# Stationary operands read with a step of two words, in a kernel of pooled attention and two feed-forward layers

## The chip, the cores and the metric

The kernel runs on one core of one Trainium2 chip. The metric is device time in microseconds (us) of one execution; the kernel before took 976.43 us, the median of three runs (975.0 to 977.66). The engines are PE (TensorE: PE for products, PEld for the loads of their stationary operands), DVE (VectorE), ACT (ScalarE), POOL (GpSimd) and SP (which issues DMAs here). L741 means line 741 of the kernel before.

## The reference

`x` has 12480 tokens of 128 channels; 32 inducing rows attend to all tokens, the tokens attend to the 32 pooled rows, and two feed-forward layers of 2048 hidden units follow. The weights are float64, all else is float32.

```python
def mab(q, kv):
    s = scale * (q @ kv.transpose(0, 2, 1))
    a = np.exp(s - s.max(-1, keepdims=True))
    a /= a.sum(-1, keepdims=True) + 1e-09
    return a @ kv
h = mab(I, x)                       # 32 pooled rows
x = mab(x, h).reshape(12480, 128)   # tokens
h = x @ moe_w_in                    # 128 x 2048
x = np.maximum(0.01 * h, h) @ moe_w_out
h = x @ moe2_w_in
return (h * (1.0 / (1.0 + np.exp(-1.702 * h)))) @ moe2_w_out
```

## The kernel before, in words

**Halves.** A float32 product is made of passes over halves in float32r, a four-byte type: `hi` holds a value's upper 12 significant bits, `lo` the rest. A product of two such values takes three passes (hi hi, lo hi, hi lo). In each pass one operand is stationary (128 x 128, loaded into PE ahead of the product) and one is moving (up to 512 columns that stream through).

**Tiles.** The tokens are cut into 25 tiles, 23 of 512 columns and the first and last of 352. The 2048 hidden units are cut into NF = 16 blocks of 128. A step is one block of one tile. The list `steps` holds first all 400 steps of the first layer (the first two tiles interleaved, four blocks at a time), then the 400 of the second. Step n issues `ffn_in` and `ffn_act` of its block, `ffn_out` of the block three steps before (LOOK = 3), and then the work that `extra` has put at this step.

**First layer.** The tokens' attention is folded into the first weights: `hw` is the product of the pooled rows and `moe_w_in`, stacked as (hi, hi, lo, lo) on the partitions' four quadrants, against the attention weights `at` as (hi, lo, hi, lo). So `ffn_in` is one product (L709, stationary `hw`). `ffn_act` makes `ghi` on ACT (L723) and `glo` on DVE (L724). `ffn_out` is three products (L741, L742, L743) with stationary blocks of `v1`, hi, lo and hi. At the end of a tile comes one product with `lin` (L745), the linear part of the leaky unit.

**Second layer.** `ffn_in` is three products (L713, L714, L715) with stationary column blocks of `w2`, hi, lo and hi; `ffn_act` is two activations on ACT (L729, L730) and a subtraction on DVE (L731); `ffn_out` is the same three products with blocks of `v2`.

**Weights.** Each weight matrix arrives as float64 bits in four blocks of 128 x 512 values. `convert_stages` makes float32 halves of one block: a load on SP's queue, magnitude on ACT (L134), clamp on POOL (L137), shift, top and bottom on DVE (L140, L145, L150; the last two read every second word of `raw`), and upper: `hi` on ACT (L155) and `lo` on POOL (L156). `matrix_in` has hi and lo in two tiles; `matrix_out` keeps a block's 128 hi words and then its 128 lo words. `w1` is only a moving operand (in `pooled_block`, L638); `v1`, `w2`, `v2` and `hw` are stationary. w1 and v1 are converted before and beside the first two tiles, w2 from step 60 on (in w1's place), v2 from step 160 on.

**hw.** `pooled_block` makes 512 columns of `hw` in PSUM, `pooled_upper` writes the hi rows (L619, ACT), `pooled_lower` the lo rows (L623, DVE), four times (b = 0 to 3). `linear_transposed` transposes hw's blocks on PE (L657), `linear_product` multiplies them with `v1` (L667), `linear_copy` and `linear_end` sum the parts into `lin`.

**Order.** It is written out by hand (`tc.manual_schedule()`): each engine runs its instructions in the order in which the program issues them, and the tables at the file's head (CONV, POOLED, LINEAR, GROUP) say at which step the work beside the layers is put. `keep_busy` issues products of zeros (bf16, 256 columns, L106) where PE would stand.

Of the kernel before, what the change touches and what calls it, by code (L numbers as in the profile page):

```python
# [10 lines left out]
F32 = mybir.dt.float32  # L11
# [7 lines left out]
P = 128  # L19
LOOK = 3  # blocks of hidden units between both products  # L20
TC = 4  # chunks of tokens in a token tile
ENDS = 88  # tokens of a chunk in the first and the last tile, 128 in the others
B = 32  # side of VectorE's transposed blocks
# [5 lines left out]
# pieces of x that blocks of weights are loaded before, the iterations of their conversion  # L29
W_LOADS = [6, 8]  # L30
W_STEPS = [0, 0, 1, 2, 2, 3]
# where the work beside the first two tiles goes, by their steps
# [14 lines left out]
def kernel(  # L47
# [10 lines left out]
    """float32 products run as float32r passes over halves: hi is a value's upper 12  # L58
    significant bits, lo = value - hi the others, both exact in float32r."""
# [23 lines left out]
    # token p * chunks + j of a part of x is row p of chunk j  # L83
# [4 lines left out]
    # token tiles that are loaded together  # L88
# [14 lines left out]
    def keep_busy(count):  # L103
        """TensorE's clock halves when it waits for long: products of zeros meanwhile."""
        for _ in range(count):
            nc.tensor.matmul(  # L106
                idle_ps[:, :256], idle[:, :P], idle[:, :256], start=True, stop=True
            )

# [1 line left out]
    CW = 512  # L111
    LOW = bits_f32(896 << 20)  # the words of 2^-127 and of float32's largest 2^127 * f
    HIGH = bits_f32((1150 << 20) | 0xFFEFF)

    def convert_stages(src, hi, lo):
        """src: [P, CW] of float64 bits. Its magnitude clamped to float32's range, sign,
        exponent and 23 fraction bits make a float32: hi is its rounding, lo the rest."""
# [42 lines left out]
    def matrix_in(src, name, tag):  # L160
        """[model, hidden]: a column block of hidden units is a stationary operand."""
        hi, lo = (wts.tile([P, DFF], F32R, name=f"{name}{h}", tag=f"{tag}{h}") for h in "hl")
# [6 lines left out]
    def matrix_out(src, name):  # L169
        """[hidden, model] by blocks of hidden units, hi and lo of a block side by side."""  # L170
        w = wts.tile([P, NF, 2, C], F32R, name=name)
        parts = []
        for o in range(0, DFF, CW):
            f = slice(o // P, (o + CW) // P)
            s = src[o : o + CW, :].bitcast(U32).rearrange("(f p) d -> p f d", p=P)
            parts.append((s, w[:, f, 0, :], w[:, f, 1, :]))
        return w, parts

    w1, w1_parts = matrix_in(moe_w_in, "w1", "w")
    v1, v1_parts = matrix_out(moe_w_out, "v1")  # L180

# [703 lines left out]
```

## Time and profile before

| | |
|---|---|
| runs | 976.43 us median (975.0, 976.43, 977.66) |
| profiled execution | span 974.8 us; its time beyond the span isn't listed, the runs' median is 1.6 us above it |
| PE busy | 963.9 us (99%), 4630 products |
| PEld busy | 783.3 us (80%), 4630 loads |
| ACT busy | 787.8 us (81%) |
| DVE busy | 644.5 us (66%) |
| POOL busy | 67.2 us (7%) |
| granted PE clock | full (2.4 GHz) in all 40 slices |
| first layer | from 47.9 us (first L709) to 433.7 us (last L745) |
| second layer | from 430.8 us (first L713) to the end |

Busy times of PE come from modelled ends, since products are pipelined: the end of one lies behind the start of the next. The distance from start to start is what a product costs in a sequence. The rows give a start, a duration, the engine, the line, the operation, out<-in by the program's names, the shape, a count, and in brackets the idle time before it with what ended it.

### The profile page before, as it was taken

The numbers are of one execution on the slowest core, as the hardware profiler recorded it, in microseconds if no ns is written. First come the engines' busy times: TensorE is split into PE (matmuls) and PEld (weight loads), VectorE is DVE, ScalarE is ACT, GpSimd is POOL, SyncE is SP. The second block draws the span as 40 slices with busy tenths as digits, with TensorE's granted clock in tenths as the row PEclk, the third lists the DMA queues.
The fourth block names the chain that finished last, engine by engine and source line by source line (L and its number), as shares of the span: only waits on it lengthen the run. The fifth ranks groups of instructions, "written<-read, shape, count | busy, mean of one in ns | idle before, by whom it ended". The sixth has DMA issues, their size and how long they took to land.

```text
span 974.8 us, 13366 instructions
## 1 busy us (share of the span) xinstructions
PE 963.9 (99%) x4630; PEld 783.3 (80%) x4630; DVE 644.5 (66%) x1049; ACT 787.8 (81%) x1378; POOL 67.2 (7%) x53
## 2 busy tenths in 40 slices
PE   9989999999999999999999999999999999999998
PEld 6667787887878878898888888888888888888887
DVE  4898788978878778765555555555555555555554
ACT  6576677767766666679999999999999999999997
POOL 1360021202200000000000000000000000000000
PEclk9999999999999999999999999999999999999999
DMA  9302120031000100000000000000000000000000
GB/s 340 98 1 55 33 65 22 7 93 33 23 23 7 27 12 23 8 1 8 12 11 12 11 12 22 11 11 11 12 12 12 11 11 18 16 12 12 12 11 19
DMA packets 15434, 27.99 MB, mean 29 GB/s; under 512 B 2358, under 2 KB 6870, under 8 KB 15366
## 3 DMA queue, kind: packets, MB, share of 16 engines
q1 hardware_dynamic: 15366, 27.14, 8.8%
q8 instruction: 36, 0.59, 0.2%
q14 instruction: 32, 0.26, 0.1%
HBM read 14.79 MB, written 6.39 MB: 22 GB/s over the span
## 4 chain that ended last, share of the span: by engine, by line
PE 96%; DVE 3%; DMA 0%; ACT 0%; issue 0%; SPq 0%; DVEq 0%; ACTq 0%
PE acc L743 18%; PE acc L742 18%; PE acc L741 18%; PE h_ps L715 9%; PE h_ps L713 9%; PE h_ps L714 9%; PE h_ps L709 9%; PE xT_ps L255 1%; DVE glo L724 1%; PE s_ps L272 1%; PE s_ps L563 1%; PE pv_ps L321 1%; PE acc L745 1%; PE p_ps L302 1%; DMA xn<-in_x_dram 0%; DVE v L145 0%
## 5 line engine op out<-in xcount | busy, mean ns | idle before, releaser
L731 DVE TENSOR_TENSOR glo<-g,ghi 128x512 fp32r<-128x512 f32 (+1 forms) x400 | 271.7, 679 | 238.9 <-ACT ghi L730 226.9
L723 ACT ACTIVATE ghi<-h_ps 128x512 fp32r<-128x512 f32 (+1 forms) x400 | 233.1, 587 | 101.6 <-PE h_ps L709 97.1
L743 PE MATMUL acc<-glo,v 128*128 128x512 f32 (+1 forms) x800 | 310.6, 388 | 0.8 <-DVE glo L724 0.6
L742 PE MATMUL acc<-ghi,v 128*128 128x512 f32 (+1 forms) x800 | 309.1, 386 | 0.5 <-POOL v L156 0.5
L741 PE MATMUL acc<-ghi,v 128*128 128x512 f32 (+1 forms) x800 | 308.2, 385 | 0.0
L724 DVE SCALAR_TENSOR_TENSOR glo<-h_ps,ghi 128x512 fp32r<-128x512 f32 (+1 forms) x400 | 263.4, 674 | 65.1 <-ACT ghi L723 61.7
L729 ACT ACTIVATE g<-h_ps 128x512 f32<-128x512 f32 (+1 forms) x400 | 234.8, 587 | 36.2 <-PE h_ps L715 0.5
L730 ACT ACTIVATE ghi<-g 128x512 fp32r<-128x512 f32 (+1 forms) x400 | 248.2, 620 | 12.6
L742 PEld LDWEIGHTS acc<-ghi,v 128*128 128x128 f32 x800 | 150.3, 188 | 33.5 <-POOL v L156 0.8
L743 PEld LDWEIGHTS acc<-glo,v 128*128 128x128 f32 x800 | 150.3, 188 | 33.2 <-DVE glo L724 3.5
L741 PEld LDWEIGHTS acc<-ghi,v 128*128 128x128 f32 x800 | 150.3, 188 | 28.6
L715 PE MATMUL h_ps<-x2l,w2h 128*128 128x512 f32 (+1 forms) x400 | 156.8, 392 | 0.0
L709 PE MATMUL h_ps<-at,hw 128*128 128x512 f32 (+1 forms) x400 | 155.4, 389 | 0.3 <-ACT at L543 0.3
L713 PE MATMUL h_ps<-x2h,w2h 128*128 128x512 f32 (+1 forms) x400 | 154.7, 387 | 0.0
L714 PE MATMUL h_ps<-x2h,w2l 128*128 128x512 f32 (+1 forms) x400 | 153.1, 383 | 0.0
L709 PEld LDWEIGHTS h_ps<-at,hw 128*128 128x128 f32 x400 | 75.1, 188 | 20.1 <-issue 3.6
L714 PEld LDWEIGHTS h_ps<-x2h,w2l 128*128 128x128 f32 x400 | 75.1, 188 | 16.1
L715 PEld LDWEIGHTS h_ps<-x2l,w2h 128*128 128x128 f32 x400 | 75.1, 188 | 15.6
L713 PEld LDWEIGHTS h_ps<-x2h,w2h 128*128 128x128 f32 x400 | 75.1, 188 | 15.5
L137 POOL TENSOR_SCALAR v<-v 128x512 f32<-128x512 f32 x16 | 31.7, 1983 | 59.3 <-ACT v L134 59.3
L759 ACT ACTIVATE x<-acc 128x512 f32<-128x512 f32 (+1 forms) x25 | 14.7, 587 | 7.7 <-PE acc L745 7.7
L762 DVE TENSOR_SCALAR o_t<-acc 128x512 f32<-128x512 f32 (+1 forms) x25 | 16.8, 671 | 0.5 <-PE acc L743 0.5
(117 smaller groups left out, 347.2 us busy)
## 6 DMA issues: line engine op xcount, KB each, us to landing
out_dram<-o_t SPq DMA_DIRECT2D x23, 256.0 KB, 2.0
xn<-in_x_dram SPq DMA_DIRECT2D x11, 512.0 KB, 9.8
raw<-in_moe_w_in_dram SPq DMA_DIRECT2D x8, 512.0 KB, 4.9
raw<-in_moe_w_out_dram SPq DMA_DIRECT2D x8, 512.0 KB, 4.2
at<-hlhi SPq DMA_DIRECT2D x44, 64.0 KB, 2.0
at<-hllo SPq DMA_DIRECT2D x44, 64.0 KB, 2.0
xn<-in_x_dram SPq DMA_DIRECT2D x2, 176.0 KB
out_dram<-o_t SPq DMA_DIRECT2D x2, 176.0 KB, 1.8
```

Source lines behind the costliest of these rows:

```text
L709: nc.tensor.matmul(o, hw[:, cols], at_t[t], start=True, stop=True)
L713: nc.tensor.matmul(o, wh[:, cols], hi, start=True, stop=False)
L714: nc.tensor.matmul(o, wl[:, cols], hi, start=False, stop=False)
L715: nc.tensor.matmul(o, wh[:, cols], lo, start=False, stop=True)
L723: nc.scalar.activation(out=hi, in_=o, func=AF.Relu)
L724: nc.vector.scalar_tensor_tensor(out=lo, in0=o, scalar=0.0, in1=hi.bitcast(F32), op0=ALU.max, op1=ALU.subtract)
L729: nc.scalar.activation(out=g, in_=o, func=AF.Silu, scale=BETA)
L730: nc.scalar.activation(out=hi, in_=g, func=AF.Copy)
L731: nc.vector.tensor_tensor(out=lo, in0=g, in1=hi.bitcast(F32), op=ALU.subtract)
L741: nc.tensor.matmul(o, v[:, f, 0, :], hi, start=(f == 0), stop=False)
L742: nc.tensor.matmul(o, v[:, f, 1, :], hi, start=False, stop=False)
L743: nc.tensor.matmul(o, v[:, f, 0, :], lo, start=False, stop=end)
```

## The change

The two halves of a value become neighbours in memory: word 2k is hi, word 2k + 1 is lo. That holds for v1, v2 (`matrix_out`) and w2 (`matrix_in` with pairs = True); w1 stays in two contiguous parts, of one tile now. `hw` has no halves side by side, so the words of two neighbouring blocks of hidden units are interleaved. Each 128 x 128 stationary operand of both layers, but for `lin`, is thereby read with a step of two words. All that writes these tiles writes with this step (L155, L156, L619, L623 of before), and `pooled_lower` takes two instructions for the two pairs of blocks. The moving operand of `linear_product` is still 256 contiguous words. Comments went too, which is left out here.

```diff
-    def matrix_in(src, name, tag):
-        hi, lo = (wts.tile([P, DFF], F32R, name=f"{name}{h}", tag=f"{tag}{h}") for h in "hl")
+    def matrix_in(src, name, tag, pairs):
+        w = wts.tile([P, 2 * DFF], F32R, name=name, tag=tag)
+        if pairs:
+            w = w.rearrange("p (d h) -> p d h", h=2)
+            hi, lo = w[:, :, 0], w[:, :, 1]
+        else:
+            hi, lo = w[:, :DFF], w[:, DFF:]
...
     def matrix_out(src, name):
-        w = wts.tile([P, NF, 2, C], F32R, name=name)
+        w = wts.tile([P, NF, C, 2], F32R, name=name)
...
-            parts.append((s, w[:, f, 0, :], w[:, f, 1, :]))
+            parts.append((s, w[:, f, :, 0], w[:, f, :, 1]))
         return w, parts
-    w1, w1_parts = matrix_in(moe_w_in, "w1", "w")
+    w1, w1_parts = matrix_in(moe_w_in, "w1", "w", False)
...
-    hw = wts.tile([P, DFF], F32R, name="hw")
+    hw = wts.tile([P, NF // 2, C, 2], F32R, name="hw")
+
+    def hw_block(f):
+        return hw[:, f // 2, :, f % 2]
+
+    def hw_out(b):
+        return hw[:, 2 * b : 2 * b + 2].rearrange("p a c k -> p a k c")
...
     def pooled_upper(b):
-        rows_upper(hw[:, b * 512 : (b + 1) * 512], hw_ps[b], 1.0)
+        rows_upper(hw_out(b), hw_ps[b].rearrange("p (a k c) -> p a k c", a=2, k=2), 1.0)
     def pooled_lower(b):
-        rows_lower(hw[:, b * 512 : (b + 1) * 512], hw_ps.pop(b), 1.0)
+        src = hw_ps.pop(b).rearrange("p (f c) -> p f c", c=C)
+        for a in range(2):
+            rows_lower(
+                hw[:, 2 * b + a].rearrange("p c k -> p k c"), src[:, 2 * a : 2 * a + 2], 1.0
+            )
...
-                ps[:, k * P : (k + 1) * P], hw[:, f * P : (f + 1) * P].bitcast(F32), ident
+                ps[:, k * P : (k + 1) * P], hw_block(f).bitcast(F32), ident
...
-                v1[:, f].rearrange("p h c -> p (h c)"),
+                v1[:, f].rearrange("p c h -> p (c h)"),
...
-        s = lin_st["s"] = main.tile([P, 2, C], F32, tag="lins", name="lins", bufs=1)
+        s = lin_st["s"] = main.tile([P, C, 2], F32, tag="lins", name="lins", bufs=1)
...
-                ps[:, :C], pair, lin_st["s"][:, h, :], start=(h == 1), stop=(h == 0)
+                ps[:, :C], pair, lin_st["s"][:, :, h], start=(h == 1), stop=(h == 0)
...
-            nc.tensor.matmul(o, hw[:, cols], at_t[t], start=True, stop=True)
+            nc.tensor.matmul(o, hw_block(f), at_t[t], start=True, stop=True)
...
-        nc.tensor.matmul(o, v[:, f, 0, :], hi, start=(f == 0), stop=False)
-        nc.tensor.matmul(o, v[:, f, 1, :], hi, start=False, stop=False)
-        nc.tensor.matmul(o, v[:, f, 0, :], lo, start=False, stop=end)
+        nc.tensor.matmul(o, v[:, f, :, 0], hi, start=(f == 0), stop=False)
+        nc.tensor.matmul(o, v[:, f, :, 1], hi, start=False, stop=False)
+        nc.tensor.matmul(o, v[:, f, :, 0], lo, start=False, stop=end)
...
-    late_matrix(matrix_in, moe2_w_in, "w2", ["w"], 60)
+    late_matrix(matrix_in, moe2_w_in, "w2", ["w", True], 60)
```

The one place where an engine's order is another is DVE's at `pooled_lower`. DVE before, at the end of the first tile's softmax (`nsum`, `na`); `hw<-hw_ps,hw` is `pooled_lower` of b = 0, `rows<-na,rows` what PE transposes next for the first tile:

```order
96 L518 RECIPROCAL nsum<-nsum 88x4
97 L519 TENSOR_TENSOR na<-na,nsum 88x128
98 L623 SCALAR_TENSOR_TENSOR hw<-hw_ps,hw 64x512
99 L529 TENSOR_TENSOR rows<-na,rows 88x8x32
100 L507 TENSOR_REDUCE nmx<-s_ps 128x4
```

The same place now (lines of the changed kernel, 5 or 17 higher):

```order
96 L523 RECIPROCAL nsum<-nsum 88x4
97 L524 TENSOR_TENSOR na<-na,nsum 88x128
98 L628 SCALAR_TENSOR_TENSOR hw<-hw_ps,hw 64x2x128 x2
99 L534 TENSOR_TENSOR rows<-na,rows 88x8x32
100 L512 TENSOR_REDUCE nmx<-s_ps 128x4
```

One instruction of 512 elements became two of 2 x 128, ahead of the subtraction that ends `rows`; the same at b = 1, 2 and 3. On PE, ACT, POOL and SP the instructions stand in the same order as before.

## Rows read from the trace of the kernel before

**Rows 1.** The page: PE's share, granted clock by slices, the chain by engine.

```profile
PE 963.9 (99%) x4630; PEld 783.3 (80%) x4630; DVE 644.5 (66%) x1049; ACT 787.8 (81%) x1378; POOL 67.2 (7%) x53
...
PEclk9999999999999999999999999999999999999999
...
PE 96%; DVE 3%; DMA 0%; ACT 0%; issue 0%; SPq 0%; DVEq 0%; ACTq 0%
```

**Rows 2.** Order of time, second layer, one step (start us, us, engine, line, operation).

```profile
599.61 0.39 PE L741 MATMUL acc<-ghi,v 128*128 128x512 f32 x1
599.62 0.19 PEld L742 LDWEIGHTS acc<-ghi,v 128*128 128x128 f32 x1
...
600.99 0.39 PE L741 MATMUL acc<-ghi,v 128*128 128x512 f32 x1
```

**Rows 3.** Order of time, first layer, ten steps of one tile.

```profile
242.18 0.39 PE L742 MATMUL acc<-ghi,v 128*128 128x512 f32 x1
...
251.34 0.39 PE L742 MATMUL acc<-ghi,v 128*128 128x512 f32 x1
```

**Rows 4.** Order of time, second layer, last tile (352 columns), three steps.

```profile
965.72 0.32 PE L713 MATMUL h_ps<-x2h,w2h 128*128 128x352 f32 x1
...
968.60 0.32 PE L713 MATMUL h_ps<-x2h,w2h 128*128 128x352 f32 x1
```

**Rows 5.** Order of time, products of zeros, one alone and eight in a row.

```profile
40.21 0.28 PE L106 MATMUL idle_ps<-idle 128*128 128x256 bf16 x1
...
41.64 1.04 PE L106 MATMUL idle_ps<-idle 128*128 128x256 bf16 x8
```

**Rows 6.** Busy time by engine in stretches (length, busy (count) each, clock, DMA).

```profile
46.00:110.00 64.00, 59.86 (x303) 46.98 (x301) 55.43 (x94) 43.89 (x84) 20.38 (x13) 1.00 0.15 41
110.00:440.00 330.00, 330.00 (x1487) 270.19 (x1486) 263.77 (x417) 234.05 (x411) 36.64 (x26) 1.00 0.10 25
440.00:975.00 535.00, 531.32 (x2354) 437.84 (x2352) 296.74 (x442) 481.77 (x808) 0.00 (x0) 1.00 0.03 13
```

**Rows 7.** Groups of loads (busy us, mean ns | idle before, by what).

```profile
L743 PEld LDWEIGHTS acc<-glo,v 128*128 128x128 f32 x800 | 150.3, 188 | 33.2 <-DVE glo L724 3.5 <-DVE glo L731 0.2
...
L321 PEld LDWEIGHTS pv_ps<-xn,pT_t 128*32 128x32 f32 x184 | 4.3, 109 | 2.0 <-issue 1.7 <-DVE nm L280 0.2
```

**Rows 8.** Groups of products by shape.

```profile
L709 PE MATMUL h_ps<-at,hw 128*128 128x512 f32 x368 | 144.9, 394 | 0.3 <-ACT at L543 0.3
L713 PE MATMUL h_ps<-x2h,w2h 128*128 128x512 f32 x368 | 144.4, 392 | 0.0
L743 PE MATMUL acc<-glo,v 128*128 128x352 f32 x64 | 21.1, 330 | 0.4 <-DVE glo L724 0.3
```

**Rows 9.** Order of time on ACT after the halves of a tile's x2.

```profile
721.04 0.61 ACT L475 ACTIVATE x2h<-x 128x512 fp32r<-128x512 f32 x1
721.57 0.58 ACT L729 ACTIVATE g<-h_ps 128x512 f32<-128x512 f32 x1
...
722.71 0.58 ACT L729 ACTIVATE g<-h_ps 128x512 f32<-128x512 f32 x1
```

**Rows 10.** Order of time on DVE at the first `pooled_lower`.

```profile
45.55 0.69 DVE L623 SCALAR_TENSOR_TENSOR hw<-hw_ps,hw 64x512 fp32r<-64x512 f32 x1
46.28 0.42 DVE L529 TENSOR_TENSOR rows<-na,rows 88x256 fp32r<-88x256 f32 x1
```

**Rows 11.** Waits of PE (total us, times, longest).

```profile
PE rows_ps L537 <- DVE rows L529: 1.9, 2, 1.7
...
PE acc L742 <- POOL v L156: 0.5, 1, 0.5
```

**Rows 12.** Groups of DVE and POOL by shape.

```profile
L145 DVE SCALAR_TENSOR_TENSOR v<-raw,v 128x512 uint32<-128x512 uint32 x16 | 11.9, 743 | 0.0
...
L724 DVE SCALAR_TENSOR_TENSOR glo<-h_ps,ghi 128x512 fp32r<-128x512 f32 x368 | 247.7, 688 | 61.1 <-ACT ghi L723 58.6
...
L156 POOL TENSOR_TENSOR v<-v,v 128x512 fp32r<-128x512 f32 x8 | 10.7, 1331 | 45.6 <-ACT v L155 45.6
```

More of the change, by code (lines that the diff above doesn't have):

```diff
@@ L673, in linear_copy @@
     def linear_copy():
-        s = lin_st["s"] = main.tile([P, 2, C], F32, tag="lins", name="lins", bufs=1)
-        nc.vector.tensor_copy(s.rearrange("p h c -> p (h c)"), lin_st["ps"][:, : 2 * C])
+        s = lin_st["s"] = main.tile([P, C, 2], F32, tag="lins", name="lins", bufs=1)
+        nc.vector.tensor_copy(s.rearrange("p c h -> p (c h)"), lin_st["ps"][:, : 2 * C])
     def linear_end():
```

## The prediction

> **What bounds the kernel now.** I read the page's engine shares, the clock strip and the chain of waits first. PE is busy 963.9 of 974.8 us, the granted clock is full in all slices (2.4 GHz), and 96% of the chain is PE [rows 1]. A busy PE is not a PE at its peak, since the ends of products are modelled; so the second view is the order of time, and in it the starts, not the lengths. In the second layer one step is six products: L741 starts at 599.61 and again at 600.99, 1.38 us later, 0.230 us a product, with no wait of PE between [rows 2]. In the first layer a step is four products: ten steps lie between L742 at 242.18 and at 251.34, so 9.16 / 40 = 0.229 us [rows 3]. In the two short tiles (352 columns), three steps of six go from 965.72 to 968.60: 2.88 / 18 = 0.160 us [rows 4].
>
> At 2.4 GHz, 512 columns take 0.2133 us and 352 take 0.1467. The rows that show what a product costs beyond its columns are the products of zeros (256 columns, bf16, 0.1067 us at 2.4 GHz): eight last 1.04 us from first start to last end and one alone 0.28, so (1.04 - 0.28) / 7 = 0.1086 us each [rows 5]. Rounded down to 0.108, 512 columns would take 0.216 us at that pace and 352 would take 0.1485. The kernel's products are 13 ns (first layer), 14 ns (second layer) and 11.5 ns (short tiles) above that. This surplus is all that a change of how the stationary operand is read can win on the main path.
>
> ACT and DVE don't make it. From the first layer's stretch to the second's, ACT's share goes from 234 / 330 = 71% to 482 / 535 = 90% and DVE's from 80% to 55% [rows 6]; the surplus moves by 1 ns. What differs between the zeros and the kernel's products lies inside PE: four bytes a column instead of two, and a stationary operand of four-byte words. Each LDWEIGHTS starts with the product before it [rows 2]. Loads of 128 columns have a mean of 188 ns, loads of 32 columns 109 [rows 7]: 79 ns for 96 columns, 0.82 ns a column, so about 105 ns of reading, beside the first half of a product that reads a column each 0.417 ns.
>
> **The change part by part.** *Loads of the stationary operand.* With contiguous words a load moves 4 bytes in 0.82 ns, the moving operand 4 bytes in 0.417 ns: the moving read runs past the load through the same partitions. With a step of two words the load moves 8 bytes in 0.82 ns, just the moving read's pace: the two keep their distance. If the surplus is what the passing costs, it goes. That is the value I take, and it is an inference: no row of before shows a load with a step. Bounds by the nearest rows: at best the whole surplus goes (0.216 and 0.1485 us a product); at worst the load needs twice its 105 ns, or loses twice as much to the moving read.
>
> Counts [rows 8]: L709 has 368 products of 512 columns, each with one of L741, L742 and L743 behind it, so 4 x 368 = 1472 in the first layer; L713 has 368, with five others each, so 6 x 368 = 2208 in the second; L743's 64 short ones are 32 a layer, so 32 x 4 + 32 x 6 = 320 short products. In 23 of the first layer the next load is `lin`, whose words stay contiguous: 1449 x 13 ns = 18.8 us; 2208 x 14 = 30.9; 320 x 11.5 = 3.7; together 53.4 us. In the stretch of the first two tiles (64 steps, 256 products) PE also stands for other reasons, 59.86 busy of 64 us [rows 6]; I count half of their 3.2 us (256 x 12.5 ns), so 51.8.
>
> Would another engine take over? After the copy of a tile's x2, ACT works without idling: L729 at 721.57, again at 722.71, so 1.14 us a step, and 721.57 - 721.04 = 0.53 for the copy once in 16 steps: 1.17 against 6 x 0.216 = 1.30 [rows 9]. DVE's 263.8 us of 330 in the first layer would be 264 of 312, 85%, with three steps of lead before its result is used. Neither does.
>
> *hw's lower half in two instructions.* L623 takes 0.69 us for 512 columns [rows 10]; the nearest row for 256 columns is L529 behind it with 0.42, so two take 0.84, 0.15 more, four times. Two of the four stand before L529, for whose rows PE waits 1.9 us [rows 11]; the others have a transposition behind them that is not late. Writes with a step of two aren't in the trace. Reads with such a step are: L145 reads every second word of `raw` and has a mean of 743 ns, against 688 for L724 over as many elements of contiguous operands [rows 12]. So 8% for a read; for a write I bound it between nothing and twice the time: 0.3 to 1.7 us for both. I take 0.5, near the read's rows.
>
> Of this the Trainium skill says otherwise: Vector Engine (DVE) Microarchitecture Reference, "5.2 Measured stream behaviour on trn2 (trn3 not measured)", has a port at its full rate only for runs of two adjacent words, and single words at about 1.7 times the time and more. By that rule L145 would take about 1.2 us, an estimate from that page; its 743 ns disagree. For PE's load the rule would speak for C below; the chance given there rests on the rows alone.
>
> *Conversion.* L155 on ACT and L156 on POOL (1331 ns [rows 12]) write with a step of two for 12 of 16 blocks. The eight of w2 and v2 are put at steps 60 and 160 onward, and their first use is step 400, so hundreds of microseconds cover them. Of v1's four blocks PE waited 0.5 us once [rows 11]; behind L156 on POOL stand the next block's clamp and a token group's subtraction. At twice the time it is at most 4 x 1.33 = 5.3 us, at least nothing; I take 0.5 by the small wait.
>
> *Without a price:* the order on PE, ACT, POOL and SP stays, w2 still takes w1's place (its last reader is at step 20), and the transpositions, the linear product and its sum have the same counts.
>
> Sum: 974.8 - 51.8 + 0.5 + 0.5 = 924.0 us for the profiled execution; the median of the runs is 1.6 us above the profile's span, so 925.6, rounded to 925.
>
> **Rivals.** *A, half of it goes:* the equal pace helps only while the two reads start well apart, or the surplus is in part the wider moving operand. For: it isn't the same in 512 and 352 columns (13.5 and 11.5), as one fixed loss per load would be. 974.8 - 26 + 1 + 1.6 = 951 us.
>
> *B, nothing moves:* the surplus belongs to four-byte products and not to the load. For: no row separates them, since all long products that aren't float32r here run at another pace or width. Against: a pure width effect would grow with the columns, and 352 / 512 of 13.5 is 9.3, not 11.5. Cost of the preparation alone: 974.8 + 1 + 1.6 = 977 us.
>
> The Trainium skill speaks for B: TensorE: Matmul & The Clock Gate, "Step-by-step: what each phase is for", has two independent read ports, so that the next load takes nothing from the running product. The same page, "Back-to-back issue gap", has 512 / 2.4 + 2.5 = 215.8 ns for a product; the zeros agree with its form (108 against 109), the kernel's 229 and 230 don't, so something takes 14 ns which the two rules together leave no room for.
>
> *C, slower, a load at half pace:* single words cost the load twice its time, 210 ns instead of 105. It decides once a load is longer than the product that hides it: below 512 columns' 229 it stays hidden, above 352 columns' 160 it doesn't. 320 x (212 - 160) = 16.6 us: 974.8 + 16.6 + 1 + 1.6 = 994 us. For: contiguous words are the only form of load in the trace. Against: DVE's reads with the same step [rows 12].
>
> *D, slower, twice the loss:* if the loss counts stretches of memory touched by the load, 128 words with a step touch twice as many, and the 53.4 us come on top instead of going: 1031 us. For: the surplus follows loads, and the change doubles the stretch that a load covers. Against: the unequal 13.5 and 11.5 for equal loads.
>
> That the change does not do what it says can be left out except for `lin` (25 products), counted above.
>
> **How the numbers follow.** The full gain has 0.42, with a range of its own of 918 to 938 us (all of the early stretch counted, or a quarter of the surplus left); A 0.17; B 0.18; C 0.12; D 0.08; preparation dearer than counted without any gain, 980 to 985 us, 0.03. A measurement here tells 0.3% (2.9 us) from no change. Faster: 0.42 + 0.17 = 0.59; same: B, 0.18; slower: 0.12 + 0.08 + 0.03 = 0.23. The range from 918 to 986 us takes in the full gain, A, B and the dear preparation and leaves out C and D, 0.20.
>
> **What would show it.** Right: starts of products in the second layer about 0.216 us apart, in the first the same, 0.149 in the short tiles; LDWEIGHTS still 188 ns; ACT in the second layer busy about 95%; L745 alone still preceded by 0.229. Wrong: 0.230 as before (B); 0.160 risen to 0.21 with LDWEIGHTS near 290 ns (C); 0.243 (D); or gaps on PE released by ACT or DVE, which would mean that the cover I counted was not there.

## The result, and the profile after

| kernel | runs | median us | range |
|---|---|---|---|
| before | 4 | 976.58 | 975.0 to 977.66 |
| after | 4 | 988.81 | 988.49 to 991.05 |

The ratio is 1.0134, with a 95% interval of 1.0118 to 1.0149: about 12 us slower, where 925 us were forecast. The span of the profiled execution went from 974.8 to 986.7 us.

The page after, in the same three lines as [rows 1]:

```profile
PE 975.7 (99%) x4630; PEld 809.5 (82%) x4630; DVE 645.2 (65%) x1053; ACT 788.1 (80%) x1378; POOL 68.0 (7%) x53
...
PEclk9999999999999999999999999999999999999999
...
PE 95%; DVE 3%; DMA 0%; ACT 0%; issue 0%; POOL 0%; SPq 0%; ACTq 0%; DVEq 0%
```

PE is busy as before, at the full clock, with as many instructions, and the chain is still PE's. So it isn't a new wait. The order of time shows where it is; first one step of the second layer (start us, us, engine, line, operation; L730 to L732 and L758 to L760 are the six products of a step), against [rows 2]:

```profile
606.47 0.40 PE L758 MATMUL acc<-ghi,v 128*128 128x512 f32 x1
606.47 0.19 PEld L759 LDWEIGHTS acc<-ghi,v 128*128 128x128 f32 x1
...
607.86 0.39 PE L758 MATMUL acc<-ghi,v 128*128 128x512 f32 x1
```

1.39 / 6 = 0.232 us. Ten steps of a first-layer tile, against [rows 3]:

```profile
246.51 0.39 PE L759 MATMUL acc<-ghi,v 128*128 128x512 f32 x1
...
255.85 0.39 PE L759 MATMUL acc<-ghi,v 128*128 128x512 f32 x1
```

9.34 / 40 = 0.2335 us instead of 0.229. Four steps of the last tile (352 columns), against [rows 4]:

```profile
976.60 0.32 PE L730 MATMUL h_ps<-x2h,w 128*128 128x352 f32 x1
...
980.49 0.32 PE L730 MATMUL h_ps<-x2h,w 128*128 128x352 f32 x1
```

3.89 / 24 = 0.162 instead of 0.160. The loads themselves, by group, against [rows 7] (busy us, mean ns):

```profile
L760 PEld LDWEIGHTS acc<-glo,v 128*128 128x128 f32 x800 | 155.7, 195 | 31.7 <-DVE glo L741 3.4 <-DVE glo L748 0.2
...
L762 PEld LDWEIGHTS acc<-at,lin 128*128 128x128 f32 x25 | 4.7, 188 | 0.9
```

A load with a step of two takes 195 ns, 7 more; `lin`, whose words stay contiguous, still takes 188, and the products beside which `lin` is loaded take 228.1 ns, against 233 for their neighbours.

To add it up I take starts alone. All 23 long tiles of the second layer (its 17th to its 385th step) take 512.1 us instead of 507.2, +4.8 with unrounded starts; 21 tiles of the first (49th to 385th step) 324.5 instead of 318.8, +5.7; everything up to the first layer's 49th step is 1.0 later, and the short tiles with the end add 0.4. That is the span's 11.9 us. The loss is spread over the products.

### The profile page after: what moved, and what is told of

Its sections match the earlier page's. It is cut to its first block, busy times and chain, and to the rows that moved or that the text cites. A ratio compares the mean times of both kernels' runs of the same rounds, so it can differ in the third digit from the quotient of the medians.

```text
span 986.7 us, 13370 instructions
## 1 busy us (share of the span) xinstructions
PE 975.7 (99%) x4630; PEld 809.5 (82%) x4630; DVE 645.2 (65%) x1053; ACT 788.1 (80%) x1378; POOL 68.0 (7%) x53
## 4 chain that ended last, share of the span: by engine, by line
PE 95%; DVE 3%; DMA 0%; ACT 0%; issue 0%; POOL 0%; SPq 0%; ACTq 0%; DVEq 0%
PE acc L760 18%; PE acc L758 18%; PE acc L759 18%; PE h_ps L730 9%; PE h_ps L731 9%; PE h_ps L732 9%; PE h_ps L726 9%; PE xT_ps L260 1%; DVE glo L741 1%; PE s_ps L277 1%; PE pv_ps L326 1%; PE acc L762 1%; PE p_ps L307 1%; PE s_ps L568 1%; DMA xn<-in_x_dram 0%
## 5 line engine op out<-in xcount | busy, mean ns | idle before, releaser
L740 ACT ACTIVATE ghi<-h_ps 128x512 fp32r<-128x512 f32 (+1 forms) x400 | 232.9, 586 | 107.6 <-PE h_ps L726 103.0
L760 PE MATMUL acc<-glo,v 128*128 128x512 f32 (+1 forms) x800 | 312.6, 391 | 1.0 <-DVE glo L741 0.9
L758 PE MATMUL acc<-ghi,v 128*128 128x512 f32 (+1 forms) x800 | 312.3, 390 | 0.0
L746 ACT ACTIVATE g<-h_ps 128x512 f32<-128x512 f32 (+1 forms) x400 | 234.3, 586 | 41.3 <-PE h_ps L732 0.6
L760 PEld LDWEIGHTS acc<-glo,v 128*128 128x128 f32 x800 | 155.7, 195 | 31.7 <-DVE glo L741 3.4
L759 PEld LDWEIGHTS acc<-ghi,v 128*128 128x128 f32 x800 | 156.1, 195 | 27.5 <-POOL v L156 0.7
L758 PEld LDWEIGHTS acc<-ghi,v 128*128 128x128 f32 x800 | 155.7, 195 | 27.7
L730 PE MATMUL h_ps<-x2h,w 128*128 128x512 f32 (+1 forms) x400 | 156.2, 391 | 0.0
L731 PE MATMUL h_ps<-x2h,w 128*128 128x512 f32 (+1 forms) x400 | 155.2, 388 | 0.0
L732 PE MATMUL h_ps<-x2l,w 128*128 128x512 f32 (+1 forms) x400 | 154.5, 386 | 0.0
L726 PEld LDWEIGHTS h_ps<-at,hw 128*128 128x128 f32 x400 | 78.0, 195 | 19.1 <-issue 3.6
L731 PEld LDWEIGHTS h_ps<-x2h,w 128*128 128x128 f32 x400 | 78.1, 195 | 14.7
L732 PEld LDWEIGHTS h_ps<-x2l,w 128*128 128x128 f32 x400 | 77.4, 194 | 14.2
L730 PEld LDWEIGHTS h_ps<-x2h,w 128*128 128x128 f32 x400 | 77.7, 194 | 13.7
```

The costliest lines, as they stand in the source:

```text
L726: nc.tensor.matmul(o, hw_block(f), at_t[t], start=True, stop=True)
L730: nc.tensor.matmul(o, wh[:, cols], hi, start=True, stop=False)
L731: nc.tensor.matmul(o, wl[:, cols], hi, start=False, stop=False)
L732: nc.tensor.matmul(o, wh[:, cols], lo, start=False, stop=True)
L740: nc.scalar.activation(out=hi, in_=o, func=AF.Relu)
L746: nc.scalar.activation(out=g, in_=o, func=AF.Silu, scale=BETA)
```

## The experiments

Ratios are set against runs of the kernel before on the same chip. "ns a product" is the mean distance of starts: in the scans over the middle of each tile, otherwise over all 512-column products that follow one another without a wait. Three of the runs are scans: they give each tile other operands than its neighbours, in one execution.

**Steps of other sizes, operands of one word.** Each tile of the second layer reads its operands in another way; what those products compute is not the reference's.

```diff
+SCAN = {1: (1, 0, 1), 2: (2, 0, 1), 3: (3, 0, 1), ... 8: (0, 0, 1), 9: (1, 0, 0), 10: (2, 0, 0), ...}
+# step and offset of the stationary operand, step of the moving one
-            nc.tensor.matmul(o, wh[:, cols], hi, start=True, stop=False)
+            wh, wl = (stationary(t, w, f * P, DFF) for w in late["w2"])
+            nc.tensor.matmul(o, wh, hi, start=True, stop=False)
```

> The kernel before, with other operands in the second layer alone (so its output is not the reference's): tile by tile the stationary operand is read with steps of 1, 2, 3, 4, 5, 6, 7, 8, 16 and 0 words, or with step 1 or 2 from a start moved by 1, 2, 4, 8 or 16 words, and in three tiles the moving operand is one word read again and again. Theory F (fetches): contiguous words are fetched two at a time, any step of two or more fetches each word alone, and each fetch beyond takes a little from the running product: all steps from 2 to 16 alike, about 234 ns a product against 230 with step 1, and LDWEIGHTS 195 against 188. Theory L (stretch of memory): the loss grows with the memory that a load spans: 234 with step 2, 241 or more with step 4, more still with 8. Theory A (addresses): the loss depends on which words meet the moving read, so odd steps or moved starts come out apart from even steps and from each other by 5 ns or more. For the surplus of 14 ns itself: if it is the meeting of both reads, it goes to about 216 ns with a moving operand of one word or a stationary one of one word; if it belongs to four-byte products as such, it stays at 229 to 230 in both.

| stationary step, words | 0 (one word) | 1 | 2 | 3 | 4 | 5 | 6 | 7 | 8 | 16 |
|---|---|---|---|---|---|---|---|---|---|---|
| ns a product | 230.8 | 230.0 | 232.3 | 233.3 | 236.7 | 237.6 | 235.6 | 238.6 | 246.1 | 233.9 |
| mean ns of a load | 189 | 188 | 194 | 253 | 309 | 305 | 306 | 314 | 330 | 301 |

Three tiles in order of time, ten steps (60 products) each: the stationary operand one word, then the moving operand one word, then that and a step of two.

```profile
612.61 0.40 PE L727 MATMUL h_ps<-x2h,w2h 128*128 128x512 f32 x1
...
626.46 0.39 PE L727 MATMUL h_ps<-x2h,w2h 128*128 128x512 f32 x1
...
634.55 0.38 PE L727 MATMUL h_ps<-x2h,w2h 128*128 128x512 f32 x1
...
647.55 0.38 PE L727 MATMUL h_ps<-x2h,w2h 128*128 128x512 f32 x1
...
655.35 0.38 PE L727 MATMUL h_ps<-x2h,w2h 128*128 128x512 f32 x1
...
668.35 0.38 PE L727 MATMUL h_ps<-x2h,w2h 128*128 128x512 f32 x1
```

13.85 / 60 = 0.231 us: with hardly any memory behind the load the surplus stays. 13.00 / 60 = 0.2167: with hardly any memory behind the moving operand it goes, and then a step of two costs nothing either. So the surplus is the moving operand's, and no layout of the load tried here wins it. The expectation had both operands' cases at 216 or both at 230; neither outcome came. The Trainium skill, TensorE: Matmul & The Clock Gate, "Back-to-back issue gap", has 512 / 2.4 + 2.5 = 215.8 ns as the gap of a single product; of the products of 512 columns only those with such a moving operand come near it. The same section's figure for a sustained stream, about 131 ns, is met by none.

The same scan also moved contiguous loads by 1 to 16 words, and got 232 to 234 ns instead of 230: the place in memory matters. That is theory A's sign, at less than the 5 ns that it named.

**v1 and v2 alone.** Their halves lie side by side; w2 and `hw` stay as before.

```diff
-        w = wts.tile([P, NF, 2, C], F32R, name=name)
+        w = wts.tile([P, NF, C, 2], F32R, name=name)
...
-        nc.tensor.matmul(o, v[:, f, 0, :], hi, start=(f == 0), stop=False)
+        nc.tensor.matmul(o, v[:, f, :, 0], hi, start=(f == 0), stop=False)
```

> Only v1 and v2 interleaved; hw and w2 contiguous as before. If the loss goes by each load with a step alone (Theories F, L and A): 2208 of 3657 loads beside long products have it, so 60% of the 12.2 us: about 983.9 us, the products ahead of L741, L742 and L743 3 to 4 ns longer and those ahead of L709, L713, L714, L715 as before. If it comes from the preparation (writes with a step, the split instruction): most of the loss gone with hw and w2, or all of it kept.

985.19 us (984.78 to 989.35), ratio 1.0108 [1.0083, 1.0133]; 233.0 ns in the first layer, 231.1 in the second. Most of the loss comes with v1 and v2. In the first layer it follows the load that runs beside a product: `hw`'s product, beside which a block of v1 is loaded with the step, takes 235.3 ns, and the last product of v1, beside which `hw` is loaded from contiguous words, 230.1. In the second layer it doesn't, against the expectation: L714, beside a contiguous load, goes from 226.0 to 231.7 ns, and L715, beside a load with the step, from 235.8 to 230.8.

**A step of four words everywhere.**

```diff
-            hi, lo = w[:, :, 0], w[:, :, 1]
+            w = w.rearrange("p (f c k h) -> p f k c h", c=P, k=2, h=2)
+            hi, lo = w[:, :, :, :, 0], w[:, :, :, :, 1]
...
-    hw = wts.tile([P, NF // 2, C, 2], F32R, name="hw")
+    hw = wts.tile([P, NF // 4, C, 4], F32R, name="hw")
```

> All stationary operands with a step of four words (words of two neighbouring blocks, hi and lo each, side by side; hw of four blocks). Theory F: as with a step of two, 987 to 991 us. Theory L: another 8 ns or more a product, 1015 us or more. Theory A: either.

1033.06 us (1031.17 to 1034.13), ratio 1.0584 [1.0568, 1.0599]. A group of loads, and seven steps of the last tile in order of time:

```profile
L735 PEld LDWEIGHTS h_ps<-x2h,w 128*128 128x128 f32 x400 | 123.9, 310 | 0.0
```

```profile
1014.74 0.40 PE L734 MATMUL h_ps<-x2h,w 128*128 128x352 f32 x1
...
1024.54 0.40 PE L734 MATMUL h_ps<-x2h,w 128*128 128x352 f32 x1
```

Loads take 310 ns instead of 188, and a product of 352 columns 9.80 / 42 = 0.233 us instead of 0.160: it no longer hides its load. This is the picture of rival C, at twice the step. The 352 columns and the 512 (0.2367) come out nearly alike, as they do where the load sets the pace. The third scan, below, bears that out: with the same step and a moving operand of 8 words, 512 columns take 0.2333 us too, instead of 0.2167.

The Trainium skill has a rule for that: SBUF — State Buffer, "Door 1: The DMA port swizzle (why `[64,N]` ≈ `[32,N]`)", speaks of lines of 16 bytes, of which two accesses must fall into each for full speed. A step of two four-byte words just meets it and a step of four misses it; 195 and 310 ns agree, and step three with 253 lies between. The same passage names a stride of 4 for this type as free, and with that the 310 ns do not agree.

**Places, and moving operands that go round.** As the first scan, with more places of contiguous loads, and moving operands that repeat their first words.

```diff
+    def moving(t, x):
+        n = SCAN[t][2]
+        if not n:
+            return x
+        return x[:, :n].rearrange("p (u k) -> p u k", u=1).to_broadcast([P, tok[t] // n, n])
```

> The kernel before with other operands in the second layer alone (its output is not the reference's). Tile by tile: the stationary operand contiguous but starting 24 to 128 words further on; the moving operand going round in its first 4, 8, 16, 32, 64, 128 or 256 words instead of through 512; and steps of two words with moved starts or with a short round. Theory M (moving stretch): the surplus of 14 ns is paid by the moving read for each new piece of memory that it enters, whoever else reads: rounds of 4 words 216 ns, and from some small round on (8 to 32 words) 230. Theory B (banks shared with others): the surplus grows slowly with the round and is full only at 256 or 512 words. For the 2 to 4 ns that the step of two words costs: if it is only that the step changed where load and moving read stand against each other, contiguous loads with moved starts reach 232 to 234 too (e1 had such cases) and steps of two with moved starts fall to 230; a start moved by 128 words, one block, must give 230 again if only the place inside a block counts. If the step costs by itself, all steps of two stay at 232 or above.

| moving operand goes round in, words | 4 | 8 | 16 | 32 | 64 | 128 | 256 | 512 (all) |
|---|---|---|---|---|---|---|---|---|
| ns a product, contiguous loads | 216.7 | 216.7 | 242.2 | 236.2 | 230.0 | 230.0 | 230.0 | 230.0 |

Loads moved by 32, 64, 96 and 128 words: 229.9 to 230.0 ns; by 24, 40, 48, 80 and 112: 232.2 to 234.4. Steps of two, moved by 0, 32, 64 and 96 words: 232.1 to 232.2 each time (the first scan had 233.1 to 233.4 with 4 and 8 words). In the second layer the pattern repeats after 32 words, 128 bytes, and the kernel before sits at its best place. Ten steps in order of time with 8 words, then with 16:

```profile
692.83 0.38 PE L729 MATMUL h_ps<-x2h,w2h 128*128 128x512 f32 x1
...
705.83 0.38 PE L729 MATMUL h_ps<-x2h,w2h 128*128 128x512 f32 x1
...
714.01 0.41 PE L729 MATMUL h_ps<-x2h,w2h 128*128 128x512 f32 x1
...
728.54 0.41 PE L729 MATMUL h_ps<-x2h,w2h 128*128 128x512 f32 x1
```

**Both layers, and one word against rounds.** The third scan, with 18 tiles of the first layer in it.

```diff
+SCAN = [{4: (2, 0, 0, 0), 5: (1, 0, 0, 0), 6: (1, 8, 0, 0), 7: (1, 16, 0, 0), ...},
+        {1: (0, 0, 16, 0), 2: (0, 0, 32, 0), 3: (0, 0, 64, 0), ... 5: (1, 0, 16, 8), ...}]
+# by layer and tile: step and offset of the stationary operand, words and start of the moving
```

> In 18 full tiles of the first layer and 23 of the second, the products read other places of the same buffers (the output is therefore not the reference's). Theory M (the surplus over 216 ns belongs to the moving operand's streaming from memory, the step of two adds its own 2 to 4 ns): a stationary operand of one word changes nothing of the odd values (moving going round in 16 words 242 ns, in 32 words 236, in 64 words 230), and in the first layer contiguous loads give 229, steps of two 232 to 235, either of them with a moving operand of 8 words 216 to 217. Theory L (the two reads collide, so that the load's own words matter): with one stationary word the 242 and 236 fall to 230 or lower. A place of the moving start that decides (M with lines of 64 bytes): moving in 16 words from word 8 gives another value than from word 0; otherwise the same within 1 ns. First layer's 4 ns more: if it is the place of the operands, moving the load by 8 to 32 words changes it by 2 ns or more; if not, all steps of two stay within 1 ns of 233.

With a stationary operand of one word the odd values stay: 243.4, 236.6 and 230.7 ns for rounds of 16, 32 and 64 words (theory M; L falls). Rounds of 16 words that start 8 words on give 243.2 instead of 242.2, rounds of 32 give 237.8 instead of 236.2. In rounds of 64 the same start counts for more, 233.4 instead of 230.0, ten steps:

```profile
590.20 0.40 PE L733 MATMUL h_ps<-x2h,w2h 128*128 128x512 f32 x1
...
604.20 0.40 PE L733 MATMUL h_ps<-x2h,w2h 128*128 128x512 f32 x1
```

14.00 / 60 = 0.2333. A load moved by 24 words, which is the same distance modulo 32 words, has the same 233.4 in the scan before. Whether the load's place is changed or the moving read's, the same distance between the two gives the same time, while what ACT and DVE read and write lies where it lay. So it is the distance between PE's two reads that counts, and not that to another engine's. Loads with a step of four beside a moving operand of 8 words, ten steps:

```profile
836.99 0.40 PE L733 MATMUL h_ps<-x2h,w2h 128*128 128x512 f32 x1
...
850.99 0.40 PE L733 MATMUL h_ps<-x2h,w2h 128*128 128x512 f32 x1
```

14.00 / 60 again, where contiguous loads gave 0.2167.

In the first layer a moving operand of 8 words gives 216.4 with contiguous loads and 216.5 with a step of two. And there the place of contiguous loads is worth more than the step:

| loads moved by, words | 0 | 4 | 8 | 16 | 24 | 32 |
|---|---|---|---|---|---|---|
| first layer, step one, ns a product | 228.9 | 232.0 | 233.3 | 227.2 | 233.4 | 233.2 |
| first layer, step two | 233.3 | | | 233.2 | | 230.3 |

**The preparation alone.** Layout, writes and splits of the changed kernel, but each stationary operand of the products is 128 contiguous words, hi and lo mixed.

```diff
-        nc.tensor.matmul(o, v[:, f, :, 0], hi, start=(f == 0), stop=False)
-        nc.tensor.matmul(o, v[:, f, :, 1], hi, start=False, stop=False)
+        x = v[:, f].rearrange("p c h -> p (c h)")
+        nc.tensor.matmul(o, x[:, :C], hi, start=(f == 0), stop=False)
+        nc.tensor.matmul(o, x[:, C:], hi, start=False, stop=False)
```

> Layout, splits and conversion of the changed kernel, but every stationary operand of products is read as 128 contiguous words (half of them hi and half lo words, so that the output is not the reference's). Theory M (all of the 12 us is the load's step): 976.0 to 978.0 us, ratio 0.999 to 1.002, products 230.0 and 229.0 ns apart. Rival P (writes with a step of two, the split of hw's lower half and the dearer conversion cost part of it): 980 us or more, with the products of the first layer still 231 ns or more apart, or with gaps in the first two tiles.

977.21 us (976.42 to 979.54), ratio 1.0004 [0.9994, 1.0014]. The long tiles' stretches are 318.8 and 507.2 us, before's to the tenth. The preparation costs nothing that can be measured; all of the 12 us is in how the loads read. Ten steps of the second layer:

```profile
542.55 0.39 PE L734 MATMUL h_ps<-x2h,w 128*128 128x512 f32 x1
...
556.35 0.39 PE L734 MATMUL h_ps<-x2h,w 128*128 128x512 f32 x1
```

13.80 / 60 = 0.230 us, as in the kernel before.

**All buffers 32 bytes further.** Distances between operands stay, absolute places change.

```diff
+    pad = const.tile([P, 8], F32, name="pad")
+    nc.vector.memset(pad, 0.0)
```

> The kernel before with 32 bytes of padding ahead of its constants, so that every buffer behind lies 32 bytes further; stationary operands begin at 64 instead of 32 bytes of each 128, moving ones at 0 instead of 96. Theory M with lines of 64 bytes: a moving operand of 512 words that begins on such a line touches 32 lines instead of 33, 0.4 ns less a product, 975.0 us, ratio 0.998. If only the distance of both operands counts: 976.5 us, ratio 1.000, 230.0 ns as before. If the stationary operand's own place counts: 232 to 234 ns a product, 983 us or more.

976.62 us, ratio 0.9999 [0.999, 1.0008], 318.8 and 507.2 us again. The distance of the two operands counts, and not their absolute place, as far as one move of 32 bytes shows it.

**Other distances, for both layouts.** If the distance decides, before and after must be compared at several. The first pair puts 64 bytes ahead of v1 and 64 behind `hw`; the others move the working buffers (attention weights, the halves of x2, `ghi`, `glo`) by 32, 64, 96 and 128 bytes away from all weights, or 64 nearer.

```diff
+    pad0 = wts.tile([P, 16], F32, name="pad0")
+    nc.vector.memset(pad0, 0.0)
     v1, v1_parts = matrix_out(moe_w_out, "v1")
...
     main = ctx.enter_context(tc.tile_pool(name="main", bufs=2))
+    pad = main.tile([P, 8], F32, tag="pad", name="pad", bufs=1)
+    nc.vector.memset(pad, 0.0)
...
-        tiny = lambda name: main.tile([P, TC], F32, tag=name, name=name, bufs=1)[:n]
+        tiny = lambda name: const.tile([P, TC], F32, tag=name, name=name, bufs=1)[:n]
```

The first hunk is the pair with pads, the second the working buffers 32 bytes further (8 words; 16, 24 and 32 for the others), the third 64 bytes nearer.

> The kernel before with 64 bytes ahead of v1 and 64 behind hw: only the distance of the first layer's two stationary matrices from its moving operands changes (modulo 128 bytes from 64 to 0), the second layer's distances stay. Theory of the place (a product's surplus depends on where the stationary words lie relative to the moving ones; in the scan 64 bytes gave 227.2 ns instead of 228.9 in the first layer): 227.2 ns in the first layer, 230.0 in the second, 1472 x 1.7 ns = 2.5 us less, 974.1 us, ratio 0.9975. Rival (the 227.2 came from that tile's own buffers): 976.6 us, ratio 1.000. If a shift in the other direction isn't the same: 231 to 234 ns, 980 to 984 us.

> The changed kernel with the same two pads. Theory of the place: a step of two reads both halves of each 128 bytes, so the distance of 64 bytes matters little: 232 to 234 ns in the first layer, 232.3 in the second, 987 to 990 us, ratio 1.011 to 1.014. Rival (the changed kernel only lies badly, and its loss is one of the place): 228 to 230 ns in the first layer, 982 us or less.

> The kernel before with its working buffers (attention output, both halves of the hidden units) 32 bytes further from all weights. Theory of the place: contiguous loads leave their best place, 231 to 234 ns a product in the first layer and up to 231 to 232 in the second, 980 to 986 us. Theory of the step alone: 229.0 and 230.0 as before, 976.5 us.

> The changed kernel with the same 32 bytes. Theory of the place: steps of two spread less with the place, 230 to 233.5 ns in the first layer and 232.0 to 232.5 in the second, 983 to 989 us; the difference to the kernel before with the same 32 bytes is then 0 to 6 us, not 12. Theory of the step alone: 12 us above it, 988.8 us.

> The kernel before with its working buffers 64 bytes further from all weights. Theory of the place, if the distance alone counts: the first layer's 232.4 ns of the two pads at v1 and hw, the second 230 to 232, 981 to 984 us. Theory of the step alone: 976.5 us.

> The changed kernel with the same 64 bytes. Theory of the place, if the distance alone counts: 231.5 ns in the first layer as with the two pads, 232 to 232.5 in the second, 984.5 to 986 us, 2 to 5 us above the kernel before with the same 64 bytes. Theory of the step alone: 12 us above it.

> The kernel before with its working buffers 96 bytes further from all weights. Theory of the place: contiguous loads away from their best place, 231 to 234 ns in the first layer, 230 to 232 in the second, 979 to 986 us. Theory of the step alone: 976.5 us.

> The changed kernel with the same 96 bytes. Theory of the place: 230 to 233.5 ns in the first layer, 232 to 232.5 in the second, 983 to 989 us, 0 to 6 us above the kernel before with the same 96 bytes. Theory of the step alone: 12 us above it.

> The kernel before with its working buffers 64 bytes nearer to all weights (two small tiles moved out of their pool). Theory of the place: in the first layer the 227.2 ns that loads moved by 64 bytes had in the scan, 1472 x 1.8 = 2.6 us less; in the second 230 to 232 ns, so 974 to 979 us. If the pattern repeats after 128 bytes: 232.9 and 232.2 ns, 987 us as 64 bytes further.

> The changed kernel with the same 64 bytes nearer. Theory of the place: 230 to 233.3 ns in the first layer (233.2 in the scan with loads moved by 64 bytes), 232 to 233 in the second, 985 to 990 us. Theory of the step alone: 12 us above the kernel before with the same 64 bytes.

> The kernel before with its working buffers 128 bytes further from all weights. If the pattern repeats after 128 bytes: 229.0 and 230.0 ns, 976.5 us. If not (loads moved by 128 bytes had 233.2 ns in the first layer's scan, 229.9 in the second's): 232 to 234 ns in the first layer, 980 to 984 us.

Times in us; "long tiles" is the sum of the two stretches from start to start (318.8 + 507.2 = 826.0 in the kernel before), which leaves out the first 100 us: the first product's start alone differs by some us between executions (46.1 to 50.9). The kernels at 32, 64, 96 and 128 ran once each; the stretches repeat well, to 0.03 us among before, the preparation alone and all buffers 32 bytes further. Differences are taken before rounding.

| distance | contiguous: run | ns, 1st / 2nd layer | long tiles | step two: run | ns, 1st / 2nd | long tiles | difference |
|---|---|---|---|---|---|---|---|
| as given | 976.6 | 229.0 / 230.0 | 826.0 | 988.8 | 233.4 / 232.2 | 836.5 | +10.5 |
| 64 nearer | 978.7 | 226.9 / 232.2 | 828.3 | 988.2 | 233.2 / 232.2 | 836.4 | +8.1 |
| pads at v1, hw | 982.2 | 232.4 / 230.7 | 832.0 | 985.5 | 231.5 / 232.2 | 834.2 | +2.2 |
| 32 further | 989.2 | 233.3 / 233.3 | 839.1 | 990.6 | 233.3 / 233.0 | 838.3 | -0.7 |
| 64 further | 987.4 | 232.9 / 232.2 | 836.1 | 988.5 | 231.4 / 232.2 | 834.2 | -1.8 |
| 96 further | 994.1 | 234.3 / 234.4 | 842.7 | 991.3 | 232.1 / 234.4 | 840.0 | -2.6 |
| 128 further | 982.8 | 233.3 / 230.0 | 831.7 | | | | |

The kernel before with 96 bytes, in order of time: ten steps of the first layer, ten of the second.

```profile
184.10 0.40 PE L711 MATMUL h_ps<-at,hw 128*128 128x512 f32 x1
...
193.47 0.40 PE L711 MATMUL h_ps<-at,hw 128*128 128x512 f32 x1
...
549.04 0.39 PE L715 MATMUL h_ps<-x2h,w2h 128*128 128x512 f32 x1
...
563.11 0.39 PE L715 MATMUL h_ps<-x2h,w2h 128*128 128x512 f32 x1
```

9.37 / 40 = 0.234 and 14.07 / 60 = 0.2345 us, with contiguous loads. The changed kernel with the same 96 bytes, second layer:

```profile
546.07 0.40 PE L732 MATMUL h_ps<-x2h,w 128*128 128x512 f32 x1
...
560.13 0.40 PE L732 MATMUL h_ps<-x2h,w 128*128 128x512 f32 x1
```

14.06 / 60, the same. And the kernel before with its buffers 64 bytes nearer, first layer:

```profile
181.21 0.39 PE L709 MATMUL h_ps<-at,hw 128*128 128x512 f32 x1
...
190.29 0.39 PE L709 MATMUL h_ps<-at,hw 128*128 128x512 f32 x1
```

9.08 / 40 = 0.227, as the third scan had it. In the second layer every distance comes out as in the scans, where a load moved towards the moving words is a moving buffer moved away: 233.3 ns at 32 bytes (233.4 with loads moved by 24 words), 232.2 at 64 (232.2, 16 words), 234.4 at 96 (234.4, 8 words), 230.0 at 128.

What follows. The kernel before loses up to 17.5 us (994.1 in its one run, against 976.6) by 96 bytes of padding alone. Contiguous loads range over 16.7 us in the long tiles, loads with a step of two over 5.8. At the given distance the contiguous layout is at the best of its seven places, and the interleaved one is not at the best of its six. With the buffers 64 bytes nearer, the step still costs 8.1 us; at the other four places the two differ by -2.6 to +2.2 us. The mean of the six differences is (10.5 + 8.1 + 2.2 - 0.7 - 1.8 - 2.6) / 6 = 2.6 us. So the 12 us are no fixed price of the step. The buffers have the same sizes and order in both kernels; what changed is the words that a load reads, and contiguous loads gain at the given distance what loads with a step of two gain at none of the six. What the step costs by itself is not shown: the mean is one of six places picked by hand. Several expectations missed: the pads at v1 and `hw` were to give 227.2 ns and gave 232.4 (equal to the scan's place within 128 bytes, but 128 bytes off: in the first layer the pattern does not repeat there, as 128 further shows with 233.3). Their second layer, which was to stay at 230.0, gave 230.7, and why is open. The kernel before at 32, 64 and 96 bytes was to take 979 to 986 us and took 987.4 to 994.1; the changed kernel at the same three was to take 983 to 989 and took 988.5 to 991.3. The step alone, 12 us at every place, held at none of the places from 32 to 96.

No version beats the kernel before. 64 bytes nearer gains 2.5 us in the first layer's stretch (316.2 instead of 318.8, before rounding) and loses 512.1 - 507.2 = 4.9 in the second's: ratio 1.0016 [1.0004, 1.0028]. Weights that lie at the one distance for the first layer and at the other for the second weren't tried.

## Why the prediction was wrong

**What bounds the kernel** was right: PE, at full clock, by the distance of starts; so was the surplus of 13 to 14 ns a product.

**The step that failed** is "the moving read runs past the load through the same partitions. [...] If the surplus is what the passing costs, it goes." The premise was an inference. With a stationary operand of one word, where there is nothing to pass, a product still takes 230.8 ns, against 230.0. The surplus belongs to the moving operand's way through memory: 216.7 ns when it stays within 8 words. So the 51.8 us of gain were never there.

**Rival B** had that cause ("the surplus belongs to four-byte products and not to the load") but not the outcome: 977 us was the price of the preparation alone, and the run with the preparation alone gives 977.2. Its counter-argument, that a pure width effect would shrink to 9.3 ns at 352 columns where 11.5 were seen, was too thin: it rested on one other width, and on a base taken from products of another type. What in the moving operand's way costs the 14 ns is open still; rounds of 16 and 32 words cost more (242 and 236 ns) than the whole operand.

**Rivals C and D** fell as to the cause. C's signs were named (loads near 290 ns, short products 0.21): loads take 195, short ones 0.160 to 0.162, and of the kernels only the one with a step of four shows C's picture. (C's price also counted 212 ns for a load that it had put at 210, which makes 0.6 us.) The measured 988.8 us lies between B's 977 and C's 994, where only the dear preparation (980 to 985) stood, and the preparation costs nothing. D's 0.243 is reached at no step below eight, in either layer (240.0 in the first at a step of four). That the product ahead of `lin` stays at 0.229 came true (0.228), but as a sign of the load's cost and not of its gain.

**What no rival had** is what decided: a product's time depends on the distance in memory between stationary and moving words, and with the step otherwise than without. Contiguous loads give 227 to 234 ns a product in the first layer and 230 to 234 in the second, loads with a step of two 230 to 233 and 232 to 234; the kernel before happens to lie near the low ends. Why the distance matters is open. The clue stood in the prediction's own numbers, and I passed it by: equal products of equal columns took 229 in one layer and 230 in the other, which I put down to nothing ("the surplus moves by 1 ns"). The trace of before had more: by unrounded starts, L714 takes 226.0 ns and L715, the next of the same step, 235.8, equal as they are; whether the distance makes that difference is not shown. A rival "the loads' new addresses are worse" would have been priced between those rows, far too small.

**The small terms** were right. `pooled_lower` in two instructions, and the group of POOL after, against [rows 10] and [rows 12]:

```profile
45.76 0.77 DVE L628 SCALAR_TENSOR_TENSOR hw<-hw_ps,hw 64x256 fp32r<-64x256 f32 x2
46.55 0.42 DVE L534 TENSOR_TENSOR rows<-na,rows 88x256 fp32r<-88x256 f32 x1
```

```profile
L156 POOL TENSOR_TENSOR w<-v,w 128x512 fp32r<-128x512 f32 x8 | 11.2, 1403 | 38.4 <-ACT w L155 38.4
...
L156 POOL TENSOR_TENSOR v<-v,v 128x512 fp32r<-128x512 f32 x8 | 10.8, 1350 | 46.8 <-ACT v L155 46.8
```

0.08 us more for the two (0.15 counted), and 1% for POOL's writes with a step into v (1350 against 1331 ns). The group of `w` holds w1's contiguous blocks too; before, its eight had a mean of 1326, and one block of w2 with 1.87 us makes most of the rise to 1403. PE's waits for them, against [rows 11]:

```profile
PE rows_ps L542 <- DVE rows L534: 2.1, 2, 1.8
...
PE acc L759 <- POOL v L156: 0.5, 1, 0.5
```

0.2 us more and the same: both covers held, as the preparation alone confirms.

## What to carry to other kernels

Before an inner stream's surplus is put down to the meeting of two operands, take each operand's memory away in turn (one word, or a few words in rounds): one run with another operand in each tile tells which of them pays. A comparison of two layouts holds for the distance between the operands at which it was made; time both at several paddings, since here 32 to 96 bytes moved an unchanged kernel by 1.1 to 1.8%, as much as the whole change. A wider step makes the load itself longer, 195 ns at two words and 310 at four, and at four a product of 352 columns no longer hides it.

## What the hardware showed that I had not expected

- A float32r product of 512 columns takes 216.7 ns when its moving operand stays within 8 words, with contiguous loads and with a step of two; in the second layer, with contiguous loads, 242 in rounds of 16 words, 236 in rounds of 32, 230 from 64 on, and nearly the same with a stationary operand of one word (243, 237, 231).
- The distance between the two operands changes a product of contiguous loads by up to 4.5 ns (2nd layer, 229.9 to 234.4) and 7.4 ns (1st layer, 226.9 to 234.3), repeating after 128 bytes in the second layer and not in the first. Moving both together by 32 bytes changes nothing (0.9999).
- A load of 128 four-byte words takes 188, 195, 253 and 310 ns at steps of one, two, three and four words, and 330 at eight.
